# Two unused tiles that shift the large SBUF buffers of a fused attention and MoE kernel to multiples of 256 bytes

## The chip, the cores and the metric

The kernel runs on one core of a Trainium2 chip. The time is device microseconds of one execution; lower is better. The engines are TensorE (PE, matmuls; PEld is its loading of weights), VectorE (DVE), ScalarE (ACT), GpSimd (POOL) and SyncE (SP, which issues the DMAs).

## The reference: what is computed

Three stages follow each other over 8 × 576 = 4,608 rows of 512 features, all in float32:

```python
# 1: attention in chunks of 64, 8 heads of 64
scores = scale * np.matmul(q_c, k_c.transpose(0, 1, 2, 4, 3))
attn = softmax(scores); out = np.matmul(attn, v_c)
# 2: x = out; layer norm, two layers, residual
ch = np.maximum(xn @ w_ch1, 0.0) @ w_ch2          # 512 -> 2048 -> 512
x = x + ch
# 3: two layers with a gate from a convolution of width 3 along the sequence
h = np.maximum(x @ w_in, 0.0)                      # 512 -> 1024
gate = 1.0 / (1.0 + np.exp(-conv_out))
return (h * gate @ w_out)                          # 1024 -> 512
```

## The kernel before, in words

The rows are cut into 36 tiles of 128 and 9 slabs of 512. The large products are done in float32 accuracy by splitting both factors into a high and a low part (float32r) and adding three matmuls: that is mm3 (L113 low × high, L114 high × low, L115 high × high). In `nc.tensor.matmul(ps, l, r)` the first factor `l` is the stationary one (128 columns, loaded as weights) and `r` the moving one, whose 256 or 512 columns are streamed out of SBUF: 4 bytes a column, so 1,024 or 2,048 contiguous bytes of each partition.

The program is written out in order; each engine takes its instructions in that order.
- Attention (class `Attention`): S and V are 64 × 64 matmuls (L384, moving operands rk and rv), P and T are 128 × 128 transposes (L424, L466, moving operand `ident`).
- Products (`product`): x @ w_ch1 by a scheme of seven block products. Stationary are the split weights `w1`, moving is `xc`, 256 columns; 9 slabs × 4 groups × 7 products × 4 × 3 matmuls. Attention of later tiles is woven in between.
- Down (`Down.down`): stationary are `hh` and `hl`, moving is w_ch2 in tiles named wd or w, 512 columns; 9 × 16 × 4 × 3 matmuls.
- Gates (`Gate`): stationary is w_in, moving is a slab of x in `xb[i % 2]`, 512 columns: even slabs i read xb0, odd ones xb1. Output tiles (`outtile`): stationary are Gh and Gl, moving is w_out, six parts in tiles named w, two in wx0 and wx1.

SBUF is given out from both ends. On the left stand first `const` (`ident`, `g_sb`, `cw_sb`, `cw_raw`, `mhalf`, `hal`), then the pools wb, wa, and after the products dp and later pb. On the right, from the top downward, stand xc, su (the tiles u), at (attention) and later pbx (xb0, wx, x2r). Nearly all tiles are whole multiples of 256 bytes per partition, so a pool's tiles share the offset at which the pool begins.

Of the kernel before, what the change touches and what calls it, by code (L numbers as in the profile page):

```python
# [8 lines left out]
F32 = mybir.dt.float32  # L9
# [35 lines left out]
def attn_moe_moe2(  # L45
# [40 lines left out]
    const = ctx.enter_context(tc.tile_pool(name="const", bufs=1))  # L86
# [14 lines left out]
    cw_raw = const.tile([128, 3 * NF2, 2], I32, name="cw_raw")  # L101
    mhalf = const.tile([128, 1], F32, name="mhalf")
    hal = const.tile([128, NF2, 2], F32, name="hal")

    def half(c):
        return slice(c * 64, c * 64 + 64)
# [413 lines left out]


    with tc.manual_schedule():
        wb_p = tc.alloc_tile_pool(name="wb", bufs=1, reuse_waits="tile")
        wa_p = tc.alloc_tile_pool(name="wa", bufs=1, reuse_waits="tile")
        xc_p = tc.alloc_tile_pool(name="xc", bufs=1, side="right", reuse_waits="tile")
# [461 lines left out]
        pb.release()  # L987
        pbx.release()
        wb_p.release()


# [41 lines left out]
```

## Time and profile before

| | before |
|---|---|
| timed runs, us | 1293.16 (median), 1291.18, 1299.48 |
| profiled execution: span, us | 1290.5 |
| TensorE busy | 1239.9 us, 96% |
| VectorE, ScalarE, GpSimd busy | 744.1, 613.9, 78.0 us |
| DMA moved | 177.70 MB, mean 138 GB/s |

The profiled execution's own time is given as its span, from the first to the last instruction; the median of the timed runs is 2.7 us above it. Matmuls overlap in TensorE's pipeline, so the duration of one is longer than the distance from its start to the start of the next. It is this distance that adds up to the time of a stage, and it is read from the starts in the timeline.

### The profile page before, as it was taken

To read this page: it belongs to the slowest core of one execution; us is meant where nothing else is said; L and a number is where in the kernel's file an instruction comes from. 1 tells how busy PE (TensorE), PEld (TensorE's weight loads), DVE (VectorE), ACT (ScalarE), POOL (GpSimd) and SP (SyncE) were. 2 spreads that over 40 slices of the span, in tenths; PEclk is the share of its full clock that TensorE was granted. 3 is DMA by queue.
4 is the path that set the end of the run, shared out by engine and by line. 5 is a ranking of instruction groups with operands and counts; after the bars stand their busy time and mean duration, and the time that the engine had idled before them with its cause. 6 is when DMAs were issued, how large, how long until landed. Compare 5 with 4: busy or idle time off the path is not lost.

```text
span 1290.5 us, 23238 instructions
## 1 busy us (share of the span) xinstructions
PE 1239.9 (96%) x9096; PEld 1080.4 (84%) x9096; DVE 744.1 (58%) x1430; ACT 613.9 (48%) x1510; POOL 78.0 (6%) x172
## 2 busy tenths in 40 slices
PE   5569999999999999999999999999999999999998
PEld 4469999999999987788888888888788888888887
DVE  7897557556565568567633443334875645665540
ACT  6776646556455345244322222222765555565541
POOL 0000000000000000000000000000121111121100
PEclk6589999999999999999999999999999999999999
DMA  9724645555454386676344445440121101211001
GB/s 269 209 103 160 209 160 186 188 175 210 158 197 151 120 284 244 189 269 234 117 143 153 163 155 179 155 162 34 33 66 58 57 18 58 66 38 36 25 25 49
DMA packets 127021, 177.70 MB, mean 138 GB/s; under 512 B 12736, under 2 KB 72128, under 8 KB 126912
## 3 DMA queue, kind: packets, MB, share of 16 engines
q1 hardware_dynamic: 126912, 176.22, 40.8%
q8 instruction: 71, 1.16, 0.4%
q14 instruction: 38, 0.31, 0.1%
HBM read 110.13 MB, written 66.06 MB: 137 GB/s over the span
## 4 chain that ended last, share of the span: by engine, by line
PE 84%; DVE 6%; DMA 5%; ACT 3%; SPq 1%; issue 1%; ACTq 0%; DVEq 0%
PE banks L113 27%; PE banks L114 26%; PE banks L115 26%; PE banks L384 3%; DMA rk<-in_k_dram 1%; DMA w<-in_moe_w_ch_dram 1%; PE banks L466 1%; DVE w L156 1%; PE banks L424 1%; DMA wd<-in_moe_w_ch_dram 1%; DVE hl L702 1%; DMA x2d<-x2T 0%; DVE w L151 0%; DVE u L159 0%; DVE w L145 0%
## 5 line engine op out<-in xcount | busy, mean ns | idle before, releaser
L113 PE MATMUL banks<-xc,w 128*128 128x256 f32 x1008 | 286.7, 284 | 11.2 <-DVE u L159 8.1
L114 PE MATMUL banks<-xc,w 128*128 128x256 f32 x1008 | 281.8, 280 | 0.0
L115 PE MATMUL banks<-xc,w 128*128 128x256 f32 x1008 | 281.7, 279 | 0.0
L701 ACT ACTIVATE hh<-hr 128x512 fp32r<-128x512 f32 x144 | 91.1, 632 | 257.0 <-PE banks L115 256.7
L702 DVE SCALAR_TENSOR_TENSOR hl<-hr,hh 128x512 fp32r<-128x512 f32 x144 | 99.3, 689 | 191.6 <-ACT hh L701 191.5
L113 PEld LDWEIGHTS banks<-xc,w 128*128 128x128 f32 x1008 | 192.1, 191 | 14.4 <-DVE u L159 8.7
L115 PEld LDWEIGHTS banks<-xc,w 128*128 128x128 f32 x1008 | 191.9, 190 | 0.0
L114 PEld LDWEIGHTS banks<-xc,w 128*128 128x128 f32 x1008 | 191.8, 190 | 0.0
L113 PE MATMUL banks<-w,hl 128*128 128x512 f32 x396 | 154.9, 391 | 0.0
L114 PE MATMUL banks<-w,hh 128*128 128x512 f32 x396 | 154.3, 390 | 0.0
L115 PE MATMUL banks<-w,hh 128*128 128x512 f32 x396 | 154.2, 389 | 0.0
L159 DVE TENSOR_TENSOR u<-banks,u 128x512 f32<-128x512 f32 x108 | 74.3, 689 | 113.6 <-ACT u L611 84.9
L917 DVE SCALAR_TENSOR_TENSOR cv<-hb,cw_sb,cv 128x510 f32<-128x510 f32 (+31 forms) x256 | 117.2, 513 | 0.6
L113 PE MATMUL banks<-xb,w 128*128 128x512 f32 x288 | 113.6, 395 | 1.8 <-ACT hb L902 1.4
L114 PE MATMUL banks<-xb,w 128*128 128x512 f32 x288 | 113.1, 393 | 0.0
L115 PE MATMUL banks<-xb,w 128*128 128x512 f32 x288 | 113.0, 392 | 0.0
L611 ACT COPY u<-banks 128x512 f32<-128x512 f32 x108 | 64.4, 596 | 99.4 <-PE banks L115 98.6
L410 ACT ACTIVATE pp<-banks,mx 128x64 f32<-128x64 f32 x288 | 86.8, 335 | 26.4 <-DVE x L438 18.7
L113 PEld LDWEIGHTS banks<-w,hl 128*128 128x128 f32 x396 | 74.4, 188 | 17.7 <-DVE hl L702 2.4
L115 PEld LDWEIGHTS banks<-w,hh 128*128 128x128 f32 x396 | 74.3, 188 | 15.5
L114 PEld LDWEIGHTS banks<-w,hh 128*128 128x128 f32 x396 | 74.3, 188 | 15.2
L904 POOL COPY hal<-hb 128x2 f32<-128x2 f32 x64 | 41.7, 652 | 730.0 <-ACT hb L902 730.0
(106 smaller groups left out, 2184.1 us busy)
## 6 DMA issues: line engine op xcount, KB each, us to landing
hd<-u SPq DMA_DIRECT2D x144, 256.0 KB, 3.2
hr<-hd SPq DMA_DIRECT2D x72, 512.0 KB, 3.7
w<-in_moe_w_ch_dram SPq DMA_DIRECT2D x27, 512.0 KB, 7.4
rv<-in_v_dram SPq DMA_DIRECT2D x36, 256.0 KB, 5.3
xd<-x SPq DMA_DIRECT2D x36, 256.0 KB, 2.2
xr<-xd SPq DMA_DIRECT2D x36, 256.0 KB, 4.2
x2d<-x2T SPq DMA_DIRECT2D x36, 256.0 KB, 2.0
x2r<-x2d SPq DMA_DIRECT2D x36, 256.0 KB, 3.7
```

Source lines behind the costliest of these rows:

```text
L113: nc.tensor.matmul(ps, ll, rh, start=first, stop=False, **kw)
L114: nc.tensor.matmul(ps, lh, rl, start=False, stop=False, **kw)
L115: nc.tensor.matmul(ps, lh, rh, start=False, stop=last, **kw)
L156: nc.vector.tensor_tensor(out=out, in0=a, in1=b, op=ALU.subtract)
L159: nc.vector.tensor_tensor(out=out, in0=a, in1=b, op=ALU.add)
L384: nc.tensor.matmul(ps[half(c), e, j, :], lt[half(e), j, c, :], rt[half(e), j, c, :], start=True, stop=True,)
L410: nc.scalar.activation(out=pp[:, j, e, :], in_=self.both[T][:, e, j, :], func=AF.Exp, scale=SCALE, bias=mx[:, e, j:j + 1], accum_out=sm[:, ...
L611: nc.scalar.copy(flat(t), bank[to])
L701: nc.scalar.activation(out=self.hh, in_=t, func=AF.Relu)
L702: nc.vector.scalar_tensor_tensor(out=self.hl, in0=t, scalar=0.0, in1=self.hh.bitcast(F32), op0=ALU.max, op1=ALU.subtract,)
L904: nc.gpsimd.tensor_copy(out=hal[:, f, :], in_=hb[:, 512:514])
L917: nc.vector.scalar_tensor_tensor(out=cv[:, a:e], in0=hb[:, a + tap:e + tap], scalar=cw_sb[:, tap, f:f + 1], in1=cv[:, a:e], op0=ALU.mult, ...
```

## The change

Two tiles of 56 float32 (224 bytes per partition) are allocated and never used: one at the end of the pool `const`, one in a new pool `edge` that is the first on the right side.

```diff
     hal = const.tile([128, NF2, 2], F32, name="hal")
+    const.tile([128, 56], F32, name="fill")
...
     with tc.manual_schedule():
+        edge = tc.alloc_tile_pool(name="edge", bufs=1, side="right", reuse_waits="tile")
+        edge.tile([128, 56], F32, name="fill")
         wb_p = tc.alloc_tile_pool(name="wb", bufs=1, reuse_waits="tile")
         wa_p = tc.alloc_tile_pool(name="wa", bufs=1, reuse_waits="tile")
         xc_p = tc.alloc_tile_pool(name="xc", bufs=1, side="right", reuse_waits="tile")
...
         wb_p.release()
+        edge.release()
```

Instructions, their order on each engine and their waits are the same in both programs; only SBUF addresses differ. The left side moves up by 224 bytes, the right side down by 224. From the memory maps of the two programs (byte address of the first tile of a name in its partition, and the remainder by 256, which its other buffers share unless it is said):

| tiles | before | after |
|---|---|---|
| `ident` | 16512 (128) | 16512 (128) |
| w1, and w_ch2, w_in, w_out in tiles w | 17440 (32) | 17664 (0) |
| hr, wd, hh, hl, cy | 132128 (32) | 132352 (0) |
| Gh, Gl | 74784 (32) | 75008 (0) |
| xb1 | 148512 (32) | 148736 (0) |
| rq, rk, rv | 132672 (64) | 132448 (96) |
| pp, pt, x (attention) | 147232 (32) | 147008 (64) |
| xn, bst | 161760 (224) | 161536 (0) |
| u | 184288 (224) | 184064 (0) |
| xb0 | 196576 (224) | 196352 (0) |
| xc | 200672 (224) | 200448 (0) |
| wx | 212960 (224) | 212736 (0) |
| x2r | 221152 (224) | 220928 (0) |
| hb, four buffers | 164896 (32, 64, 96, 128) | 165120 (0, 32, 64, 96) |
| cv, three buffers | 173216 (160, 192, 224) | 173440 (128, 160, 192) |
| gt, two buffers | 179456 (0, 32) | 179680 (224, 0) |
| ob | 183616 (64) | 183840 (32) |

## Rows read from the trace of the kernel before

**Rows 1.** The page: busy time, and slices of the span.

```profile
PE 1239.9 (96%) x9096; PEld 1080.4 (84%) x9096; DVE 744.1 (58%) x1430; ACT 613.9 (48%) x1510; POOL 78.0 (6%) x172
...
PEclk6589999999999999999999999999999999999999
```

**Rows 2.** Windows of products, down, gates: busy us (instructions) by engine, clock, DMA share, GB/s.

```profile
core 0: us, PE busy (x) PEld busy (x) DVE busy (x) ACT busy (x) POOL busy (x), PEclk, DMA share, GB/s
...
100.00:200.00 100.00, 100.00 (x1351) 98.95 (x1346) 62.38 (x137) 58.74 (x222) 5.99 (x10) 1.00 0.53 183
...
600.00:800.00 200.00, 199.85 (x882) 165.20 (x881) 87.22 (x136) 55.30 (x90) 0.00 (x0) 1.00 0.49 161
...
1000.00:1100.00 100.00, 100.00 (x437) 81.77 (x437) 59.34 (x130) 54.21 (x101) 15.96 (x36) 1.00 0.14 45
```

**Rows 3.** Waits of TensorE, 100 to 1290 us: total, times, longest us.

```profile
PE banks L113 <- DVE u L159: 2.7, 2, 1.6
PE banks L113 <- ACT u L611: 2.1, 1, 2.1
PE banks L113 <- ACT hb L902: 1.4, 2, 1.2
PE banks L113 <- DVE hl L702: 0.6, 2, 0.5
```

**Rows 4.** TensorE's groups by shape: out<-moving,stationary xcount | busy us, mean ns.

```profile
L114 PE MATMUL banks<-xc,w 128*128 128x256 f32 x1008 | 281.8, 280 | 0.0
L114 PE MATMUL banks<-w,hh 128*128 128x512 f32 x396 | 154.3, 390 | 0.0
...
L114 PE MATMUL banks<-xb,w 128*128 128x512 f32 x288 | 113.1, 393 | 0.0
...
L114 PE MATMUL banks<-w,Gh 128*128 128x512 f32 x216 | 84.4, 391 | 0.0
...
L114 PE MATMUL banks<-wd,hh 128*128 128x512 f32 x180 | 70.2, 390 | 0.0
...
L114 PE MATMUL banks<-wx,Gh 128*128 128x512 f32 x72 | 28.4, 395 | 0.0
L384 PE MATMUL banks<-rk,rq 64*64 64x64 f32 x1152 | 26.2, 238 | 15.5 <-DMA rk<-in_k_dram 14.9
L384 PE MATMUL banks<-rv,pt 64*64 64x64 f32 x1152 | 24.4, 238 | 7.1 <-ACT pt L430 7.0
```

**Rows 5.** Timeline of TensorE, products: start us, us; 31 rows, first and last.

```profile
299.79 0.28 PE L113 MATMUL banks<-xc,w 128*128 128x256 f32 x1
...
303.19 0.28 PE L113 MATMUL banks<-xc,w 128*128 128x256 f32 x1
```

**Rows 6.** Timeline of TensorE, output tile and gate of slab 2: 12, 6, 24 steps.

```profile
971.08 0.39 PE L113 MATMUL banks<-w,Gl 128*128 128x512 f32 x1
...
973.80 0.40 PE L113 MATMUL banks<-wx,Gl 128*128 128x512 f32 x1
...
975.20 0.40 PE L113 MATMUL banks<-xb,w 128*128 128x512 f32 x1
...
980.80 0.39 PE L113 MATMUL banks<-w,Gl 128*128 128x512 f32 x1
```

**Rows 7.** The same for a gate of slab 3: 16 steps from the first row.

```profile
1010.09 0.39 PE L115 MATMUL banks<-xb,w 128*128 128x512 f32 x1
...
1013.72 0.39 PE L113 MATMUL banks<-w,Gl 128*128 128x512 f32 x1
```

**Rows 8.** Cold products: timeline (8 steps), window with clock, windows of L113.

```profile
46.12 0.41 PE L113 MATMUL banks<-xc,w 128*128 128x256 f32 x1
...
47.83 0.42 PE L115 MATMUL banks<-xc,w 128*128 128x256 f32 x1
...
44.00:48.00 4.00, 3.44 (x16) 0.50 1.05 297
...
100.00:500.00 400.00, 274.40 (x970) 1.00 0.55 191
```

**Rows 9.** The chain that ended last, 100 to 130 us: start us, us, what.

```profile
109.44 0.87 PE banks L424 x8
...
122.38 2.02 PE banks L384 x128
```

**Rows 10.** Tile gt: duration ns min/median/max, first and last start.

```profile
L932 DVE SCALAR_TENSOR_TENSOR gt<-cv,hb x72: 683/692/696, 900.1 to 1261.0; 128x512 f32<-128x512 f32 x56, 128x511 f32<-128x511 f32 x8, 128x513 f32<-128x513 f32 x8
```

**Rows 11.** Chain and windows where DMA stands on the path.

```profile
41.02 6.20 DMA rk<-in_k_dram
...
47.88 10.13 DMA rk<-in_k_dram
...
0.00:60.00 60.00, 31.16 (x389) 23.98 (x390) 46.84 (x96) 40.51 (x130) 3.62 (x12) 0.60 0.86 246
...
450.00:500.00 50.00, 45.21 (x352) 42.89 (x351) 31.74 (x53) 24.17 (x42) 0.00 (x0) 1.00 0.84 300
```

## The prediction

> **What bounds the kernel now.** The page's first two parts come first: TensorE (PE) is busy for 96% of the span, at clock 1.00 (2.4 GHz) from slice 4 on [rows 1]. The table of windows shows the same by stage, with VectorE (DVE) at 44 to 62%, ScalarE (ACT) at 28 to 59% and DMA at 0.14 to 0.53 [rows 2]. The list of waits says how much of the rest is idle: from 100 us to the end TensorE waited 6.8 us in all [rows 3]. So the time after 100 us is the sum of TensorE's start-to-start steps, and whatever changes a step changes the end.
>
> Most of these steps are the three matmuls of mm3 (L113 to L115); the groups by shape give the counts [rows 4]: 3,024 of 256 columns (the products) and 3,456 of 512 columns (down 3 × (396 + 180) = 1,728; gates 3 × 288 = 864; output tiles 3 × 216 = 648 from w and 3 × 72 = 216 from wx). The durations there (280 to 395 ns) overlap and are no price. The price is the step in the timeline:
> - 256 columns, moving operand xc (224 past a multiple of 256 bytes): 30 steps from 299.79 to 303.19, 113.3 ns [rows 5].
> - 512 columns from w in an output tile (32 past): 971.08 to 973.80, 12 steps, 226.7 ns; the six from wx that follow (224 past): 233.3 ns; the 24 of a gate from xb0 (224 past): 975.20 to 980.80, 233.3 ns [rows 6].
> - The same gate matmuls with the same weights, but from xb1 (32 past), as slabs 1, 3, 5, 7 have it: 1010.09 to 1013.72, 16 steps, 226.9 ns [rows 7].
>
> Two things follow. An equal matmul costs 6.6 ns more from one address than from another, so the address matters here. And none runs at a column per clock: 256 clocks of 2.4 GHz are 106.7 ns, 512 are 213.3. That the array itself needs no more is shown by the cold stretch: at clock 0.50 the same xc matmuls, at the same addresses, step 1.71 / 8 = 213.8 ns [rows 8], which is 256 clocks of 1.2 GHz (213.3). At half clock nothing is lost; at full clock 6.6 ns are. What is lost is therefore not the array's work but the supply of the moving operand, at about 9 bytes per ns and partition. In clocks of 2.4 GHz the steps are 272, 544 and 560, that is 17, 34 and 35 times 16 clocks; 16 clocks stream 64 bytes. A row of 1,024 bytes that begins 32 past a multiple of 64 touches 17 pieces of 64 bytes; one that begins on the multiple touches 16. The 256-column step is just that count; 2,048 bytes would touch 33, and take 34 or 35.
>
> **The change, part by part.** The fillers are never written or read: no instruction, no DMA, no wait is added, and every engine keeps its order. Only addresses move.
>
> *Products.* xc goes from 224 to 0. Of the 1,008 triples, 970 run after 100 us [rows 8], 2,910 matmuls. Cost afterwards: at least 106.7 (a column per clock), at most 113.3 (no better). No row shows a matmul of mm3 that begins at 0. The nearest is the transposes, whose moving operand ident begins 128 past, a multiple of 64: eight take 0.87 us, 109 ns each [rows 9], which I read as 128 columns streamed twice, 256 clocks plus 2.3 ns. They draw half the bytes per clock, so they are a weak witness for the supply, but a good one for what a matmul costs besides its columns. I take 106.7 + 2.3 = 109.0: 2,910 × 4.3 = 12.5 us.
>
> *512 columns.* Between 213.3 and 226.7 (0 no better than 32). I take 213.3 + 2.3 = 215.6. Down: 1,728 × 11.1 = 19.2 us. Gates of odd slabs: 4 × 96 = 384 × 11.1 = 4.3; of even slabs: 480 × 17.7 = 8.5. Output tiles: 648 × 11.1 = 7.2 and 216 × 17.7 = 3.8. Sum 43.0 us.
>
> The Trainium skill (TensorE: Matmul & The Clock Gate, "Back-to-back issue gap") gives a warm step as the columns over 2.4 GHz plus about 2.5 ns, whatever the address: 109.2 and 215.8 ns. By that price the saving is estimated at 54 us, close to the sum here, but the rows above are 4 to 18 ns over the page's steps, so the page leaves today's kernel unexplained.
>
> *Attention.* rq, rk and rv go from 64 to 96, off the multiple of 64. 128 matmul records of L384 take 2.02 us [rows 9], 15.8 ns each; there are 2 × 1,152 [rows 4], 36 us in all. If their rows of 256 bytes lose what xc's lose now (113.3 against 109.0, 4%), that is 1.4 us; the bounds are 0 and 3 us (8%, as 233.3 against 215.6). I take 1 us, as loss.
>
> *ScalarE and VectorE.* gt's two buffers begin at 0 and at 32 in the kernel before, and the writes into both last 683 to 696 ns with the median at 692 [rows 10]; an offset effect of over 2% isn't there. Cost nothing, and both engines have their slack as cover [rows 2].
>
> *DMA.* On the path it stands before 60 us, with loads of rk of 6 and 10 us [rows 11], and rk begins on no multiple of 256 before or after. The w loads go from 32 to 0. The stretch of 60 us runs at DMA share 0.86 [rows 11]; a 1% change of it would be 0.5 us. I take 0, bounds -0.5 and +0.5.
>
> *What is late next.* TensorE arriving 4 to 8% sooner meets evacuations by engines that are busy 62% at most in these stages, so nearly all of the gain should stand. The exception is the join at 450 to 500 us, where DMA is at 0.84 and TensorE already idles [rows 11]; I give back 2 us there, 0 to 6.
>
> Sum: -12.5 - 43.0 + 1 + 2 = -52.5 us. The profiled execution has a span of 1290.5, 2.7 under the median of the three timed runs (1293.16); what lies around the span doesn't change. 1293.2 - 52.5 = 1240.7, say **1241 us**. Bounds of the main case: every step at a column per clock is another 2,910 × 2.3 + 3,456 × 2.3 = 14.6 us, 1226, which needs a matmul without any cost of its own; with attention at +3 and 6 us given back, 1247.
>
> **Rivals.**
> - *One piece of 64 bytes less, not two or three* (34 and 35 become 33): 512 columns at 220.0 ns. Saving 2,760 × 6.7 + 696 × 13.3 + 12.5 = 40.3, less 3: 1256 us. For it: the steps are whole multiples of 16 clocks. Against: 2,048 aligned bytes are 32 pieces.
> - *0 is no better than 32, the change does nothing.* All the dear operands (xc, xb0, wx) also lie at the top of the memory, above 196,000, all the cheap ones under 174,000, and the change leaves that as it is; the 17 pieces may be 16 and one of handling per 1,024 bytes, at any address. Then at most the 6.6 ns of 224 against 32 go: 696 × 6.6 = 4.6 us, 1289 to 1293 us. Against: the stretch at half clock, and 34 being twice 17 while 224 shifts only the 512-column step. The Trainium skill (SBUF — State Buffer, "Door 1: The DMA port swizzle") speaks for this rival: it gives lines of 16 bytes, and 32, 64 and 224 are all multiples of 16, so every buffer would already be aligned. The difference of xb0 and xb1 isn't explained by such lines.
> - *Slower.* Weights and moving operands begin at the same offset after the change, where products now read 32 beside 224. If streams that start together collide, steps could rise to the dearest seen, 233.3 from 226.7: 2,760 × 6.6 = +18.2 us, 1311. It is over 1% from +3.8 ns per 512-column step. Against: hl and w2 both begin at 32 and have the cheaper step.
>
> **Chances.** Main case 0.48, one piece less 0.22, nothing 0.22, slower 0.08. A measurement of this kernel tells about 1% (13 us) from no change: faster 0.70, same 0.22, slower 0.08. The range from 1228 holds the main case but for its extreme, the second, and, up to 1290, half of the third: 0.8.
>
> **What would show it.** In the profile of the changed kernel: xc steps of 109 (113 if wrong), steps of 216 in down, and xb0 and xb1 equal (if they still differ by 6.6, it is the place in the memory and not the offset); L384's 128 records at 2.0 to 2.1 us; span of the gate stages shorter by 5 to 8%, the first 60 us unchanged. Wrong would be: steps that don't move, or a new wait of TensorE for DVE, ACT or a DMA in the list of waits.

## The result, and the profile after

The changed kernel is slower: 1301.12 us median (1299.10 to 1303.18, 20 runs) against 1292.36 (1290.30 to 1301.52, 20 runs) of the kernel before, a ratio of the mean times of 1.0058 with an interval of 1.0045 to 1.0072. Four of the 20 runs before took 1299.5 to 1301.5 us and the others 1290.3 to 1293.6, so the ratio of the medians is larger, 1.0068. The profiled execution has a span of 1300.5 us against 1290.5, so 10.0 us are to be found. The forecast was 1241 us, 1228 to 1290.

The page of the changed kernel, its busy times and clock, answers to [rows 1]. All line numbers of mm3 are one higher (L114 to L116), and those behind the pool edge three (L705 was L702).

```profile
span 1300.5 us, 23238 instructions
...
PE 1251.4 (96%) x9096; PEld 1097.7 (84%) x9096; DVE 744.6 (57%) x1430; ACT 614.7 (47%) x1510; POOL 78.6 (6%) x172
...
PEclk6689999999999999999999999999999999999999
```

TensorE is as full as before and at the same clock; the other engines' busy times are the same. Its waits from 100 us on add up to 5.7 us, against 6.8 [rows 3] (engine line, releaser: total us, times, longest):

```profile
PE banks L114 <- ACT hb L905: 1.9, 2, 1.2
PE banks L114 <- DVE u L160: 1.7, 2, 1.4
PE banks L114 <- ACT u L614: 1.4, 1, 1.4
PE banks L114 <- DVE hl L705: 0.7, 3, 0.4
```

No new wait appeared and none went, so the 10 us have to be in the steps. The timeline of TensorE shows them, as [rows 5] did for products (20 steps between these two rows):

```profile
299.63 0.28 PE L114 MATMUL banks<-xc,w 128*128 128x256 f32 x1
...
302.03 0.28 PE L116 MATMUL banks<-xc,w 128*128 128x256 f32 x1
```

2.40 us for 20 steps is 120.0 ns, where it was 113.3. For a gate of an even slab, read from xb0 (24 steps; [rows 6] had 233.3 ns):

```profile
989.13 0.39 PE L114 MATMUL banks<-xb,w 128*128 128x512 f32 x1
...
994.57 0.39 PE L114 MATMUL banks<-w,Gl 128*128 128x512 f32 x1
```

5.44 / 24 is 226.7 ns, the step that output tiles from w and gates of odd slabs had already [rows 6, 7]. Both slabs' gates now have it: over all steps under 240 ns the mean is 226.8 ns from xb0 and 227.2 from xb1.

Where the time goes is seen at the borders of the stages. For one tile, the rows give duration in ns (min/median/max) and the start of the first and the last of its matmuls. Before, the high × low matmuls of down and of the gates:

```profile
L114 PE MATMUL banks<-wd,hh x180: 388/390/402, 490.8 to 855.9; 128*128 128x512 f32 x180
L114 PE MATMUL banks<-xb,w x288: 387/394/399, 886.5 to 1247.6; 128*128 128x512 f32 x144
```

After:

```profile
L115 PE MATMUL banks<-wd,hh x180: 387/389/402, 505.6 to 870.6; 128*128 128x512 f32 x180
L115 PE MATMUL banks<-xb,w x288: 387/389/402, 901.2 to 1258.0; 128*128 128x512 f32 x144
```

Down begins 14.8 us later, the gates 14.7 us later, and the last gate 10.4 us later: the products lose, down is unchanged, the gates win a part back. Adding up all steps from 88.8 us on, from one start to the next, gives the whole account, in us (differences taken before rounding):

| steps from | count | before | after | difference |
|---|---|---|---|---|
| xc (products) | 2,883 | 344.1 | 358.4 | +14.4 |
| w, wd against hh, hl (down) | 1,728 | 395.7 | 395.6 | -0.1 |
| xb0 (gates of even slabs) | 480 | 113.8 | 111.2 | -2.6 |
| xb1 (gates of odd slabs) | 384 | 88.8 | 88.5 | -0.2 |
| w against Gh, Gl (output tiles) | 648 | 147.3 | 146.9 | -0.4 |
| wx against Gh, Gl | 215 | 50.2 | 48.7 | -1.4 |
| attention's 64 × 64 matmuls | 1,856 | 30.8 | 31.2 | +0.3 |

With +0.1 us for the transposes that is +10.0 us. The row of the products holds more than their steps. Between matmuls of products that follow each other directly (under 130 ns, from 103 us on) the mean step went from 114.0 to 120.0 ns, which is 17.2 us for the 2,868 products after 100 us; about 3 us come off again in shorter waits (the two on u: 4.8 us before, 3.1 after) and in fewer long steps beside other work. And about 1.0 us of the 10.0 is clock: in both kernels TensorE waits 3.7 us, up to 97.5 us from the start, and begins again at a granted clock of 0.50 (1.2 GHz); it is 1.00 (2.4 GHz) from 100.5 us on before and only from 102.9 us on after. That is all of attention's +0.3 (its steps from 103 us on add up to 27.4 us in both) and 0.7 us of the products (the first seven steps after 101 us took 0.92 and 1.64 us).

The first 60 us, where [rows 11] has loads of rk on the path, are as they were: the two loads take 6.71 and 9.55 us, 16.3 us together as before, at the same 246 GB/s.

```profile
40.47 6.71 DMA rk<-in_k_dram
...
48.54 9.55 DMA rk<-in_k_dram
```

### The profile page after: what moved, and what is told of

It reads as the page before. It is cut to its first block, busy times and chain, and to the rows that moved or that the text cites. A ratio compares the mean times of both kernels' runs of the same rounds, so it can differ in the third digit from the quotient of the medians.

```text
span 1300.5 us, 23238 instructions
## 1 busy us (share of the span) xinstructions
PE 1251.4 (96%) x9096; PEld 1097.7 (84%) x9096; DVE 744.6 (57%) x1430; ACT 614.7 (47%) x1510; POOL 78.6 (6%) x172
## 4 chain that ended last, share of the span: by engine, by line
PE 86%; DVE 5%; DMA 4%; ACT 3%; SPq 1%; issue 1%; ACTq 0%; DVEq 0%
PE banks L114 27%; PE banks L115 27%; PE banks L116 27%; PE banks L385 3%; DMA rk<-in_k_dram 2%; PE banks L467 1%; DMA w<-in_moe_w_ch_dram 1%; PE banks L425 1%; DVE w L157 1%; DMA wd<-in_moe_w_ch_dram 1%; DVE hl L705 1%; DMA x2d<-x2T 0%; DVE w L152 0%; SPq L366 0%; DVE xr L160 0%
## 5 line engine op out<-in xcount | busy, mean ns | idle before, releaser
L114 PE MATMUL banks<-xc,w 128*128 128x256 f32 x1008 | 291.7, 289 | 9.6 <-DVE u L160 6.9
L115 PE MATMUL banks<-xc,w 128*128 128x256 f32 x1008 | 287.4, 285 | 0.0
L116 PE MATMUL banks<-xc,w 128*128 128x256 f32 x1008 | 287.2, 285 | 0.0
L705 DVE SCALAR_TENSOR_TENSOR hl<-hr,hh 128x512 fp32r<-128x512 f32 x144 | 99.3, 689 | 191.5 <-ACT hh L704 189.1
L114 PEld LDWEIGHTS banks<-xc,w 128*128 128x128 f32 x1008 | 195.8, 194 | 12.1 <-DVE u L160 7.5
L115 PEld LDWEIGHTS banks<-xc,w 128*128 128x128 f32 x1008 | 196.0, 194 | 0.0
L116 PEld LDWEIGHTS banks<-xc,w 128*128 128x128 f32 x1008 | 195.6, 194 | 0.0
L114 PE MATMUL banks<-w,hl 128*128 128x512 f32 x396 | 154.8, 391 | 0.0
L116 PE MATMUL banks<-w,hh 128*128 128x512 f32 x396 | 154.1, 389 | 0.0
L114 PE MATMUL banks<-xb,w 128*128 128x512 f32 x288 | 112.7, 391 | 2.2 <-ACT hb L905 1.9
L116 PE MATMUL banks<-xb,w 128*128 128x512 f32 x288 | 112.1, 389 | 0.0
L114 PEld LDWEIGHTS banks<-w,hl 128*128 128x128 f32 x396 | 74.3, 188 | 17.6 <-DVE hl L705 2.4
L116 PEld LDWEIGHTS banks<-w,hh 128*128 128x128 f32 x396 | 74.3, 188 | 15.4
```

Of the source, the lines that this page charges most:

```text
L114: nc.tensor.matmul(ps, ll, rh, start=first, stop=False, **kw)
L115: nc.tensor.matmul(ps, lh, rl, start=False, stop=False, **kw)
L116: nc.tensor.matmul(ps, lh, rh, start=False, stop=last, **kw)
L705: nc.vector.scalar_tensor_tensor(out=self.hl, in0=t, scalar=0.0, in1=self.hh.bitcast(F32), op0=ALU.max, op1=ALU.subtract,)
```

## The experiments

The account asks one question: why does 0 make the 512-column steps cheap and the 256-column step dear? In the kernel before two things were mixed up. What read from 32 past a multiple of 256 had its weights (the stationary operand) at 32 as well, so a distance of 0; what read from 224 (xc, xb0, wx) had its weights at 32, a distance of 192. The change made every distance 0. Theory A is that this distance sets the step, theory B that the moving operand's own offset does, theory C that its place in the memory does.

**Each filler alone, and matmuls alone at chosen offsets.** left_only leaves out the pool edge:

```diff
     const.tile([128, 56], F32, name="fill")
...
-        edge = tc.alloc_tile_pool(name="edge", bufs=1, side="right", reuse_waits="tile")
-        edge.tile([128, 56], F32, name="fill")
...
-        edge.release()
```

> Only the filler in const: weights, down's operands, Gh, Gl and xb1 begin at 0, while xc, xb0 and wx stay at 224. Theory A: xc is 224 beyond its weights instead of 192 (before) or 0 (after), so its step is whatever the offsets run shows for 224, and equal to that of right_only; operands that are both on the left keep 226.7. Theory B: xc 113.3, xb0 and wx 233.3, as in the kernel before, 1292 us. Theory C: as in the kernel before, 1292 us.

right_only leaves out the filler in const:

```diff
-    const.tile([128, 56], F32, name="fill")
```

> Only the pool edge: xc, xb0 and wx begin at 0, the weights and all that is on the left stay at 32, attention's rq, rk, rv go to 96. Theory A: xc is 32 short of its weights, by 256 the same distance as in left_only, so equal steps and an equal time (but for attention) with left_only. Theory B: xc 120, xb0 and wx 226.7, as in the changed kernel, 1301 us. Theory C: 1292 us.

m1_offsets is a kernel of matmuls alone, the core of which is:

```python
w = sta[:, i % 4 * 256 + s // 4:][:, :128]
nc.tensor.matmul(banks[:, i // 64 % 4, out:out + n], w, mov[:, m // 4:m // 4 + n], start=True, stop=True)
```

Here m and s are the start offsets of the moving and the stationary operand in bytes, n is the number of columns, i counts the matmuls and out is 0.

> Matmuls alone: one moving tile and one stationary tile, both at a multiple of 512 bytes, 24 matmuls of 512 (then 256) columns for each pair of start offsets; the moving offset goes from 0 to 1024, the stationary one is 0 or a few others. Nothing of the reference is computed. Theory A (the step depends on the distance between the moving operand and the weights that are loaded beside it): equal distances give equal steps, (0,0) = (32,32) = (64,64) = (128,128) = (256,256), with 120 ns for 256 columns and 226.7 for 512 at distance 0, and 113.3 and 233.3 at distance 192; other distances give other steps, some of them perhaps with nothing lost (109 and 216). Theory B (the moving operand's own offset sets it): the step at moving offset 0 is 120 and 226.7 whatever the stationary offset, and at 32 the same as at (32,0). Theory C (the place in the memory): 256 columns step alike at all offsets.

Both halves are slower than the kernel before: left_only 1302.47 us, ratio 1.0070 (1.0053 to 1.0087), right_only 1303.07 us, ratio 1.0079 (1.0064 to 1.0094), against 1293.39. Theory B wanted 1292 for left_only, theory C for both; B's 1301 for right_only came near, but its steps did not, since B wanted the 226.7 ns of the changed kernel for the gates. The windows of products and of gates (us, TensorE busy and its number of matmuls, clock, DMA share, GB/s) show the two halves alike. Left_only:

```profile
140.00:400.00 260.00, 260.00 (x3414) 1.00 0.52 178
...
1000.00:1100.00 100.00, 100.00 (x437) 1.00 0.14 45
```

right_only:

```profile
140.00:400.00 260.00, 260.00 (x3415) 1.00 0.52 178
...
1000.00:1100.00 100.00, 100.00 (x437) 1.00 0.14 48
```

The same window of products in the kernel before:

```profile
140.00:400.00 260.00, 260.00 (x3474) 1.00 0.53 182
```

and both windows in the changed one:

```profile
140.00:400.00 260.00, 260.00 (x3390) 1.00 0.52 176
...
1000.00:1100.00 100.00, 100.00 (x443) 1.00 0.14 49
```

The gates have 437 matmuls in both halves, as in the kernel before [rows 2], so xb0 kept its dear step although it begins at 0 in right_only. From the starts, the mean step between products that follow each other directly is 118.3 ns in left_only and in right_only, where it was 114.0 before and is 120.0 after. All products together take 353.4 and 355.7 us (344.1 before, 358.4 after); the 2.3 us between the halves lie in the waits on u, which are 2.9 and 5.3 us. So xc at 224 with weights at 0, the offset that it had before, is dear, and xc at 0 with weights at 32 just as much: by 256 both stand at a distance of 224.

The matmuls alone give a map in steps of 32 bytes, read at granted clock 1.00. Mean steps in ns from the starts, without the first four of each group; "(m, s)" are the offsets of the moving and the stationary operand:

| distance m - s | 0 | 32 | 64 | 96 | 128 | 160 | 192 | 224 | 256 | 448 |
|---|---|---|---|---|---|---|---|---|---|---|
| 256 columns | 120.0 | 117.7 | 117.7 | 119.7 | 118.6 | 117.4 | 113.3 | 118.2 | 119.9 | 113.3 |
| 512 columns | 226.7 | 233.3 | 228.9 | 233.7 | 233.5 | 234.3 | 233.3 | 233.3 | 226.9 | 233.4 |

Equal distances at other addresses: 512 columns (32, 32) 226.9, (64, 64) 226.7, (128, 128) 226.7, (256, 256) 226.7; 256 columns (32, 32) 120.0, (256, 256) 120.0, and (0, 64), distance 192, 113.5. (The first 48 matmuls hold the cold start and aren't read.) The map repeats after 256 bytes, with exceptions for 256 columns. At a distance of 192 the groups at m = 192 and 448 took 113.3 ns throughout, but those at m = 704 and 960, which are the same distance modulo 256, took 117.7: the distance has two steps, and what decides between them isn't known. And (0, 128) and (0, 96) took 120.1 and 118.6 ns, where the other groups at their distances, 128 and 160, took 118.5 to 118.8 and 117.4. With the moving operand at 0 throughout, the step goes from 120.0 to 118.3 and 113.5 as the weights alone go from 0 to 32 and 64, which neither B nor C allows. So theory A holds in the main, and B and C fall. Two things in the map matter for this kernel. The best distance of the multiples of 32 is another one for each length: 192 for 256 columns, 0 for 512. And no distance reaches 109 or 216 ns, the steps that the forecast counted on.

**The distances held, the offsets changed; and the reverse.** same_distance keeps the filler in const and shrinks the other to 32 bytes; zero_distance has no filler on the left and 192 bytes on the right (both against the changed kernel):

```diff
-        edge.tile([128, 56], F32, name="fill")
+        edge.tile([128, 8], F32, name="fill")      # same_distance
+        edge.tile([128, 48], F32, name="fill")     # zero_distance, without the filler in const
```

> The filler in const as in the change (left side at 0), but the pool edge holds 32 bytes instead of 224: xc, xb0 and wx begin at 192, so every distance between moving operand and weights is that of the kernel before, at other addresses, and the left side begins at multiples of 256. Theory A: steps as before (xc 113.3, xb0 and wx 233.3, the left ones 226.7) and no change of the time, 1291 to 1295 us. Theory B (multiples of 256 as such do harm): near the changed kernel or left_only, 1300 us.

> The complement of same_distance: one filler of 192 bytes on the right, ahead of all pools there, and none on the left. xc, xb0 and wx begin at 32 as their weights do, so every distance is that of the changed kernel (0), but no large buffer on the left or of these begins at a multiple of 256; rq, rk, rv begin at 128. Theory A: xc 120 ns, xb0 and wx 226.7, time as the changed kernel, 1299 to 1303 us. Theory B (multiples of 256 as such do harm): as before, 1292 us, or 1288 with the gain of xb0 and wx.

same_distance takes 1293.06 us against 1293.87, ratio 0.9980 (0.9958 to 1.0002): with nearly the whole left side on multiples of 256, no change that these runs can tell. zero_distance takes 1302.62 us against 1293.20, ratio 1.0060 (1.0031 to 1.0089): the changed kernel's time without its multiples of 256. Windows of same_distance:

```profile
140.00:400.00 260.00, 260.00 (x3481) 1.00 0.53 182
...
1000.00:1100.00 100.00, 100.00 (x438) 1.00 0.14 45
```

and of zero_distance:

```profile
140.00:400.00 260.00, 260.00 (x3389) 1.00 0.51 175
...
1000.00:1100.00 100.00, 100.00 (x443) 1.00 0.16 52
```

3,481 beside 3,474 before, 3,389 beside 3,390 after; 438 beside 437 in the gates [rows 2], 443 beside 443. The mean steps of the products say the same: 114.3 ns in same_distance beside 114.0 before, 120.0 in zero_distance beside 120.0 after. The alignment to 256 by itself does nothing that can be seen here; the distance accounts for the change.

**Each length at its own best distance.** If that is so, the gain of the gates can be had without the loss of the products: xc stays, and only the pool that comes after the products is moved.

```diff
+        edge = tc.alloc_tile_pool(name="edge", bufs=1, side="right", reuse_waits="tile")
+        edge.tile([128, 48], F32, name="fill")
         pbx = tc.alloc_tile_pool(name="pbx", bufs=1, side="right", reuse_waits="tile")
...
+        edge.release()
```

> The kernel before, with one filler of 192 bytes on the right ahead of the pool pbx, after the products: xb0 and wx begin at 32 as their weights do (distance 0), xc keeps its 192. Theory A: xb0 and wx step 226.7 instead of 233.3: 696 x 6.6 = 4.6 us less, 1288.5 us, ratio 0.9965. Theories B and C: no change at 32, 1293 us.

1288.53 us against 1293.87, ratio 0.9952 (0.9927 to 0.9976), 5.3 us between the medians where theory A gave 4.6, and faster than both kernels. The gates have the changed kernel's 443 matmuls in 100 us:

```profile
140.00:400.00 260.00, 260.00 (x3422) 1.00 0.53 179
...
1000.00:1100.00 100.00, 100.00 (x443) 1.00 0.14 45
```

Its window of products has 3,422 and not 3,474, and its profiled span is 1293.8 us, 3.3 us above that of the kernel before, although xc and its weights stand where they did. This is the second step that m1_offsets showed at a distance of 192: the products ran at a mean of 117.6 ns here. That cost 7.8 us in the products, while gates and output tiles took 4.7 us less. The kernel before has the second step in stretches, as here (17 steps in 2.00 us, 117.6 ns, beside the 113.3 of [rows 5]):

```profile
119.86 0.28 PE L114 MATMUL banks<-xc,w 128*128 128x256 f32 x1
...
121.86 0.28 PE L113 MATMUL banks<-xc,w 128*128 128x256 f32 x1
```

All products at 117.6 instead of 113.3 ns would be 2,883 × 4.3 = 12 us, so by this estimate a kernel with its products at a distance of 192 can take up to that much more in one execution than in another. At distance 0 the step was 120 ns in 2,735 of the 2,868 cases after 100 us.

**What collides.** Two more kernels of matmuls alone ask whether it is the loading of weights beside the stream.

> Matmuls alone again, nothing of the reference is computed: distances of 16, 48, 80 .. 240 bytes; pairs of matmuls whose weights lie at 0 and 64 in turn (moving at 0), or whose moving operands lie at 0 and 192 in turn (weights at 0); stationary operands of 128, 64 and 32 columns; bfloat16 operands. Theory A1 (a matmul is slowed by the weights of the next one, which are loaded while it streams): with moving at 0 and weights at 0 and 64 in turn, the 256-column step is 113 ns where the next weights lie at 64 and 120 where they lie at 0; with fewer stationary columns the extra time shrinks, to under half at 32 columns, toward 109 and 216 ns; bfloat16 halves the bytes and the steps fall to about 109 and 216 at every distance. Theory A2 (the matmul's own weights): the other way round in the pairs, and the extra time stays with fewer stationary columns. Theory D (the loss is a fixed handling of the moving rows and the distance only shifts it): no fall with fewer stationary columns.

> Matmuls alone, nothing of the reference is computed: 640 of 256 columns and 384 of 512, the start of the moving operand and that of the weights drawn at random out of 0, 64, 128 and 192; then 32 each with both drawn together at distance 0 and at distance 192. Read by averages of the step over each pair of neighbours. Theory A1 (the next matmul's weights count): the spread is over the distance between a matmul's moving operand and the next one's weights, some 5 ns between the best and the worst, and 1 ns or less over the distance to its own weights. Theory A2: the other way round. If neither spread is over 2 ns, a row only settles into its step when the same distance repeats. With distance held and addresses drawn: 120 and 227 at 0, 113 to 118 and 233 at 192 if the distance of a matmul's own operands is enough.

m2_weights, mean steps in ns, with 128, 64 and 32 stationary columns:

| moving offset, weights at 0 | 128 | 64 | 32 |
|---|---|---|---|
| 256 columns at 0 | 120.0 | 113.4 | 113.4 |
| 256 columns at 192 | 117.8 | 119.1 | 116.6 |
| 512 columns at 0 | 227.7 | 230.2 | 231.7 |
| 512 columns at 192 | 233.2 | 232.7 | 231.6 |

A second group of 256 columns at 192, with 128 stationary ones, took 113.3: again the two steps. Fewer weights shift the step. Only in the first row does the extra time over 109 ns fall to under half, as theory A1 wanted for every row, and there 64 columns do as much as 32; in the others it falls by less than 2 ns or grows, which is nearer to theory D's "no fall". With weights at 0 and 64 in turn (moving at 0) 256 columns take 117.5 where the next weights are at 64 and 119.2 where they are at 0; neither 113 nor 120, so neither theory A1 nor A2 is borne out. With moving operands at 0 and 192 in turn (weights at 0) 256 columns take 117.0 and 116.8, and 512 columns 228.4 and 225.0: the average, 226.7, is that of distance 0, though every second matmul stands at 192. Distances of 16, 48, 80 to 240 give 115.1 to 119.3 ns for 256 columns and 230.8 to 234.8 for 512, nothing better; at 16 the step was 118.5 here and 113.4 in m1_offsets, so 192 is not the only distance with two steps. bfloat16 operands are free of it, 109.2 and 215.8 ns at distances 0, 64 and 192. In the timeline (start, duration, merged) its 72 matmuls of 512 and 72 of 256 columns stand as one row, where 72 × (215.8 + 109.2) would be 23.4 us:

```profile
161.64 23.57 PE L51 MATMUL banks<-mob,stb 128*128 128x512 bf16 x144
```

m3_random, offsets drawn at random: 117.9 ns on average for 256 columns and 231.8 for 512. Sorted by the distance to the matmul's own weights the averages lie between 117.8 and 118.0, by the distance to the next one's between 117.6 and 118.3; for 512 columns 231.2 to 232.7 and 231.5 to 232.2. With the distance held and the addresses drawn, 256 columns take 119.3 ns at 0 and 118.3 at 192, scattered between 112 and 128, and 512 columns 230.9 and 232.0. So no single pair of operands sets a step, and an equal distance alone doesn't either. A row of matmuls settles into 113, 120, 227 or 233 ns at distances of 0 and 192 when the same offsets repeat, modulo 256, from matmul to matmul, as they do in the kernel. What the streams contend for stays open; that the loading of the weights is one of the two sides is suggested by the moves with s and not shown.

## Why the prediction was wrong

*What bounds the kernel* held: TensorE's steps are the time, no wait took over, and DMA, ScalarE and VectorE cost nothing, as forecast. That the address matters held too, and the test that was named for it came out as named: xb0 and xb1 are equal after, so for the 512-column gates it was no matter of the place in the memory.

*The price of a step from offset 0* is the step that failed. The loss was put down to the supply of the moving operand alone, by its own offset, so that offset 0 had to be better than 32 and 224; the step was put at 109.0 and 215.6 ns, from the transposes of [rows 9]. The runs show that the distance to the weights counts, and the steps are 120.0 and 226.7 ns, 18 and 34 times 16 clocks. That the steps before fitted a count of 64-byte pieces was a coincidence: a row at 0 touches fewer pieces than at 224 and takes longer. The transposes, said to be a weak witness, were one: by the prediction's reading they draw half the bytes per clock, and the bfloat16 matmuls, with half the bytes per column, step at 109.2 and 215.8 ns at all three distances that were tried.

- Products: -12.5 us forecast, +14.4 measured. Going from 224 to 0 took xc from distance 192 to 0, the best of the map's multiples of 32 to nearly the worst. (The 2,910 matmuls of this term are 2,868: the 970 triples that the window counts after 100 us hold 14 of down. That is 0.2 us.)
- 512 columns: -43.0 forecast, -4.8 measured. Down, the odd gates and the output tiles from w stood at distance 0 before and still do; only xb0 and wx won some 6.6 ns a step, 4.1 us together, near the 4.6 us that the rival "0 is no better than 32" gave.
- Attention: +1 forecast, none measured: the +0.3 us of the table is the clock, and 128 records take 2.02 us as before.
- Given back at the join: 2 forecast, not put to the test, since TensorE came there later and not sooner.

The profile of the kernel before had the confounding in it. Every operand that was compared as "32 past" also stood at distance 0, every one "224 past" at 192, and the one hint that length and offset don't act alike (224 costs 256 columns one unit of 16 clocks, 512 columns three, 32 costs two) was explained away. The rival "slower" named the right condition, streams that start at the same offset, but with 0.08, and on the 512-column steps, whose best distance is just that; the step it forgot is the 256-column one. Its 1311 us and the 1301 measured are near each other by luck. As no row showed a product at distance 0, its bound should have reached above 113.3, to about as much above as 233.3 lies over 226.7.

The step that the forecast was weighed against fared so. The Trainium skill's step (TensorE: Matmul & The Clock Gate, "Back-to-back issue gap", where it is the gap of a single matmul, with no word on addresses), 109.2 and 215.8 ns, is met exactly by bfloat16 here, 109.2 and 215.8, and by no settled float32r step of 256 or 512 columns. And the Trainium skill (SBUF — State Buffer, "Who interferes with whom") gives TensorE two independent read ports, one for the moving operand and one for the loading of weights; that the step of a float32r matmul goes from 120.0 to 113.5 ns as its weights alone move from 0 to 64 is at odds with that independence, and the measurement decides.

## What to carry to other kernels

For float32r matmuls that follow each other without a gap, look at the distance modulo 256 bytes between the moving operand and the stationary one, not at alignment: 6.6 ns a step, 3 to 6%, hung on it here, and the best distance was 0 for 512 columns and 192 for 256 (where the step can also be 117.6). This holds where the same offsets repeat from matmul to matmul. Before a change of layout, list for each kind of matmul both offsets before and after, and leave alone what already stands well; a filler ahead of one pool moves that pool alone. If two quantities move together in all rows of a profile, as offset and distance did here, the rows can't say which of them acts, and the range has to hold both answers, on both sides.

## What was not expected of the hardware

- Where a float32r step settles it is a whole multiple of 16 clocks of 2.4 GHz: 272 and 288 for 256 columns, 416 for 384 (173.3 ns), 544 and 560 for 512. The second step at a distance of 192, 117.6 ns, is 282 and fits no such multiple. bfloat16 takes 262 and 518.
- 128 columns of float32r take 111.5 to 111.8 ns at the five moving offsets tried (0 to 256 in steps of 64, weights at 0), nearly as long as 256, so a float32r matmul of 128 columns gains only 2 to 8 ns over one of 256.
- At distance 192, 256-column matmuls run for long stretches at 113.3 or at 117.6 ns with nothing else changed: steps of 116.5 to 119 ns are 313 of 2,868 in the profile of the kernel before and 2,655 in that of xb_wx_at_32.
